# A branch around an attention: the unused side's code moved in front of the used one, and two masks moved inside

## The chip, the cores and the metric

The kernel runs on one core of a Trainium2 chip. The core has five engines that run side by side, each with its own instruction stream: TensorE (PE in the profile; its weight loads are PEld), VectorE (DVE), ScalarE (ACT), GpSimd (POOL) and SyncE (SP), which here only issues transfers. Each engine takes its instructions in order and waits on semaphores for the others. The metric is the device time of one execution in microseconds (us); lower is better.

## What is computed

The reference runs two stages. The first is causal attention with a sliding window and sink tokens, over 4 batches, 8 heads, 768 positions and head size 64; `n_sink` (4) and `window` (128) are inputs that the kernel reads at run time. The second is a mixture of 8 experts with sticky routing: a token keeps the expert of the token before it unless a local gate is below one half.

```python
scores = scale * np.matmul(q, k.transpose(0, 1, 3, 2))
keep = (pos[None, :] < n_sink) | ((rel >= 0) & (rel < window))    # rel = query - key position
a = softmax(np.where(keep, scores, -1e9))
x = np.matmul(a, v)                                               # then heads side by side: [B, S, 512]

for each batch, for each position s:
    fresh_e = argmax(x[s] @ w_gate)
    e = fresh_e if s == 0 or sigmoid(x[s] @ w_local) < 0.5 else prev_e
    out[s] = softmax(x[s] @ w_gate)[e] * (relu(x[s] @ w1[e]) @ w2[e])
```

## The kernel before

**Two attentions, one branch.** Because `n_sink` and `window` are known only at run time, the kernel holds two versions of the attention, both made by `attention(fast)`. The usual one, `attention(True)`, is for narrow masks: a window of 1 to 128 and at most 8 sinks. It looks, for each block of 128 queries, only at the block's own keys, at those of the block before it, and at 8 sink keys. The general one, `attention(False)`, looks at all 768 keys and works for any values. VectorE computes a flag from the two numbers (lines 180 to 191), every engine loads it into a register (`values_load`, line 212), and each engine takes its own branch (`tc.If(narrow != 0)`, line 834). With the inputs of the reference the usual side is taken. Both sides are unrolled code, and both stand one after the other in each engine's instruction stream: the usual one directly behind the branch, the general one behind it. The usual side therefore ends with a jump past the general one. That jump is also recorded under line 834.

**Before the branch.** SyncE and ScalarE issue the first loads (lines 87 to 161); they include queries and keys of the first two head pairs, first their leading 256 columns, then the rest. TensorE runs warm-up matmuls (line 173). VectorE makes three additive masks in one tile (lines 194 to 204): `mask2`, 264 columns wide, for blocks 2 to 5 (keys of the block before, 8 sinks, own keys), `mask1`, 256 columns, for block 1, and `mask0`, 128 columns, for block 0. A kept place has 0 in the mask and every other one -3e38. `rel` is the distance of query and key and `key` the number of the sink key, both loaded tables.

**Splitting queries and keys.** The scores are computed from high and low halves: a number is rounded to the matmul's format (the high half, line 120) and the remainder is the low half (line 125). For each pair of heads `qk_split` gives two steps, keys and queries. In group 0 (`SENG`) the key's high half is VectorE's, its low half GpSimd's, the query's high half ScalarE's and its low half VectorE's. The first pair's leading columns (`lead0[0:2]`) are split ahead of the branch, the second pair's (`lead0[2:]`, line 743) right behind it, and the remaining columns (`rest0`) two steps each at the ends of blocks 0 and 1.

**Inside the usual side.** There are 48 blocks (4 batches, 2 groups of 4 heads, 6 blocks of queries), in a software pipeline with an order written out by hand for TensorE, VectorE and ScalarE (`tc.manual_schedule`); SyncE's and GpSimd's order is left to the scheduler. In step n, block n is scored and evicted, block n-1 is transposed, block n-2 is multiplied with the values, and block n-3 is finished:

- `score` (line 548): six matmuls for each of the two head pairs: high by high, high by low, low by high.
- `out` (lines 560 and 563): for each of a pair's two heads VectorE evicts the scores from PSUM, adds the mask and takes the row's extreme, and ScalarE takes the exponential. `out(now[0])` is the first pair, `out(now[1])` the second.
- `turn` and `turned` (578, 585), `apply` (614), `back` (504) and `finish` (520, 524): transposition, product with the values, and division by the sum.

Routing of a finished batch (lines 248 to 342) is interleaved; its last part, for half of the last batch, comes behind the branch.

**Behind the branch.** The first expert's first 256 tokens are already fetched and transposed at the end of the usual side (`early_prep`, lines 384 to 390: ScalarE's copy is the high half of `x_a`, VectorE's subtraction at line 390 the low half). What follows is common to both sides. TensorE begins with the first layer of expert 0 (line 1000): 24 matmuls for two slices of the hidden size, then the transposes of the late routing (line 280), which need VectorE's `fk` (lines 265 and 266), then more slices. SyncE's first transfer there is a weight load (line 866). The experts are run by a sequence of switches (recorded under line 1295), each a jump to one of 25 unrolled arms.

Of the kernel before, what the change touches and what calls it, by code (L numbers as in the profile page):

```python
# [15 lines left out]
ALU = mybir.AluOpType  # L16
# [3 lines left out]
P = 128  # L20
# [7 lines left out]
SK = 8  # L28
# [5 lines left out]
BIG = 3.0e38  # L34
# [4 lines left out]
N2 = 2 * P + SK  # L39
# [27 lines left out]
def kernel(ctx, tc, qkd, vn, vs, w1, w2, nw, c_misc, c_ident, c_idw, c_small,  # L67
                                          c_all, out):
    nc = tc.nc
# [23 lines left out]
    rel, key = misc[:, 0:N2], misc[:, N2:N2 + SK]  # L93
# [75 lines left out]
    with tc.tile_pool(name="ps_w", bufs=1, space=PS) as ps_w:  # L169
        wt = ps_w.tile([P, 512], F32, name="wt")  # L170
        zb = zrow.bitcast(BF16)
        for _ in range(WARM):
# [11 lines left out]
                                   op0=ALU.mult, op1=ALU.add)  # L184
    nsk, win = scal[:, 0:1], scal[:, 1:2]
# [6 lines left out]
                                             op0=ALU.is_le, op1=ALU.mult)  # L192

    mask = at.tile([P, N2 + 3 * P], F32, name="mask")
    mask2, mask1, mask0 = mask[:, 0:N2], mask[:, N2:N2 + 2 * P], mask[:, N2 + 2 * P:]
    nc.vector.tensor_scalar(mask2, rel, win, None, op0=ALU.is_lt)
    nc.vector.scalar_tensor_tensor(out=mask2, in0=rel, scalar=0.0, in1=mask2, op0=ALU.is_ge, op1=ALU.mult)
    nc.vector.tensor_scalar(mask2[:, P:P + SK], key, nsk, None, op0=ALU.is_lt)
    nc.vector.tensor_copy(mask1[:, 0:P], mask2[:, 0:P])
    nc.vector.tensor_copy(mask1[:, P:2 * P], mask2[:, P + SK:N2])  # L200
    nc.vector.tensor_copy(mask0, mask2[:, P + SK:N2])
    for m in (mask1, mask0):
        nc.vector.tensor_tensor(out=m[:, 0:SK], in0=m[:, 0:SK], in1=mask2[:, P:P + SK], op=ALU.max)
    nc.vector.tensor_scalar(mask, mask, BIG, -BIG, op0=ALU.mult, op1=ALU.add)

    lead0, heads0 = qk_split(0, SENG, False, slice(0, lead), slice(0, lead))
    rest0 = qk_split(0, SENG, False, slice(lead, S), slice(lead, KPAD))[0]
    with tc.issue_after(flag_op.ins) if FLAGF else ExitStack():
        for f in lead0[0:2]:
            f()  # L210

    narrow = nc.values_load(flag_i[0:1, 0:1], min_val=0, max_val=1,
                            skip_runtime_bounds_check_because="a product of comparisons")
# [19 lines left out]
    def setup():  # L233
        nc.sync.dma_start(xs[0:P, :], zrow)
        nc.gpsimd.tensor_copy(identb, ident)
        nc.scalar.copy(base_r, base_f)
# [164 lines left out]
    def xb_meta(b):  # L401
        xb = xb_t[b % 2]
        nc.gpsimd.tensor_copy(xb.bitcast(I32)[:, :, DM + 1], ids[:, b * NBLK:(b + 1) * NBLK])
        nc.gpsimd.memset(xb[:, :, DM + 2:ROW], 0.0)
# [50 lines left out]
    def attention(fast):  # L455
        sfx = "f" if fast else "g"
        with ExitStack() as st:
# [40 lines left out]
            def collect(blk, n):  # L498
                blk["xt"] = t = p2.tile([P, NPR, P], F32, tag="xt", name=f"xt{n}")
                blk["out"] = nc.vector.tensor_copy(t, blk["avt"])  # L500
# [12 lines left out]
            def invert(blk):  # L513
                nc.vector.reciprocal(blk["rs"], blk["rs"])
# [14 lines left out]
            def spans(i):  # L529
                if i == 0:  # L530
                    return P, 0, mask0, ((0, 0),)
                if i == 1:
                    return 2 * P, 0, mask1, ((0, 0), (1, P))
                return N2, koff(i - 1), mask2, ((i - 1, 0), (i, P + SK))

            def score(u):
                b, g, i, c, heads = u["b"], u["g"], u["i"], u["c"], u["heads"]
                w, off, mk, tiles = spans(i)
                n = f"{sfx}{b}_{g}_{i}_{c}"
                if c == 0:  # L540
                    u["blk"]["pe"] = pe_p.tile([P, HG, N2], F32, tag="pe", name=f"pe{n}")
                    u["blk"]["z"], u["blk"]["n"] = sum_z[:, ((b * G + g) * NBLK + i) % NZ], n
                u["bias"] = p3.tile([P, 2], F32, tag="bias", name=f"bias{n}")
                sps = ps_s.tile([P, 2, 512], F32, tag="s", name=f"s{n}")

                for m, (qx, kx) in enumerate(heads[c]):
                    for t in range(2):
                        u["mm"] = nc.tensor.matmul(sps[:, t, :w], qx[ROWS[t], i * P:(i + 1) * P],  # L548
                                                   kx[ROWS[t], off:off + w], start=m == 0, stop=m == 2)
                u["sps"] = sps  # L550

            def out(u):
                i, c = u["i"], u["c"]
                w, off, mk, tiles = spans(i)
                n = f"{sfx}{u['b']}_{u['g']}_{i}_{c}"
                pe, z, bias, sps = u["blk"]["pe"], u["blk"]["z"], u["bias"], u["sps"]
                for t in range(2):
                    h = 2 * c + t
                    sm = p3.tile([P, N2], F32, tag="sm", bufs=4, name=f"sm{n}_{t}")
                    u["dve"] = nc.vector.tensor_tensor_reduce(out=sm[:, :w], in0=sps[:, t, :w], in1=mk, scale=-0.125,  # L560
                                                              scalar=BIG, op0=ALU.add, op1=ALU.min,
                                                              accum_out=bias[:, t:t + 1])
                    nc.scalar.activation(pe[:, h, :w], sm[:, :w], AF.Exp, bias=bias[:, t:t + 1], scale=-1.0,  # L563
                                         accum_out=z[:, h, 0:1])

            def pack(blk, n):
                blk["pk"] = pk = p2.tile([P, 3, HG, SK], F32, tag="pk", name=f"pk{n}")
                nc.vector.tensor_copy(pk, blk["pe"][:, :, P:P + SK].unsqueeze(1).broadcast_to([P, 3, HG, SK]))

            def turn(u):  # L570
                b, g, i, c = u["b"], u["g"], u["i"], u["c"]
                w, off, mk, tiles = spans(i)
                n = f"{sfx}{b}_{g}_{i}_{c}"
                nt, pe = len(tiles), u["blk"]["pe"]
                tp = ps_t.tile([P, 2, 2, P], F32, tag="t", name=f"tp{n}")
                for t in range(2):
                    for k, (j, o) in enumerate(tiles):
                        nc.tensor.transpose(tp[:, t, k, :], pe[:, 2 * c + t, o:o + P], ident)  # L578
                u["tp"] = tp
# [105 lines left out]
            if fast:  # L685
# [62 lines left out]
                for n in range(nb + 3):  # L748
                    now, a, z, y = (blocks[x] if 0 <= x < nb else [] for x in (n, n - 1, n - 2, n - 3))
                    nm = f"{sfx}{n}"  # L750
                    deep = bool(a) and a[0]["i"] >= 2
                    for u in now:
                        if u["k"] == 0 and u["g"] == 0 and n:
                            xb_meta(u["b"])
                        if u["gi"] == 0 and u["k"] == 6:
                            xb_meta(0)
                            setup()
                        u["heads"] = u["prep"]["heads"]
                        score(u)
                    if deep:  # L760
                        pack(a[0]["blk"], nm)
                    if y:
                        collect(y[0]["blk"], nm)
                    if now:
                        out(now[0])
                    for u in a:
                        turn(u)
                    if deep or y:
                        bk = ps_b.tile([P, 512], F32, tag="b", name=f"bk{nm}")
                    if deep:  # L770
                        tps = sink_turn(a[0]["blk"], bk)
                    mm = back(y[0]["g"], y[0]["blk"], bk) if y else None
                    if a:
                        turned(a[0])
                    lo = sink_out(a[0]["blk"], tps, mm, nm) if deep else None
                    if now:
                        out(now[1])
                    if a:
                        turned(a[1])
                        sums(a[0]["blk"])  # L780
                    if y:
                        finish(y[0]["b"], y[0]["g"], y[0]["i"], y[0]["blk"], bk, nm)
                    if deep:
                        lo()
                    if a:
                        invert(a[0]["blk"])
                    if n < 2:
                        for f in rest0[2 * n:2 * n + 2]:
                            f()
                    for u in now:  # L790
                        slot(u, u["gi"], u["k"])
                    if y:
                        done(y[0]["b"], y[0]["g"], y[0]["i"])
                    if z:
                        apply(z, nm)
                    weights(n, now[0] if now else None)
                    for _ in range((ENDING if n >= nb - 2 * NBLK + 2 else STEPS).get(
                            n if n >= nb - 2 * NBLK + 2 else n % (2 * NBLK), 0)):
                        step()
# [31 lines left out]
            while pend:  # L831
                step()

    with tc.If(narrow != 0) as branch:
        attention(True)
    with branch.Else():
        attention(False)
# [461 lines left out]
```

## Time and profile before

| what | us |
|---|---|
| runs shown | 606.99, 608.37, 1598.67 |
| their median | 608.37 |
| time of the profiled execution | 606.81 |
| span of the profiled execution, first to last instruction | 605.0 |
| busy in it: TensorE | 541.8 (90%) |
| VectorE | 354.4 (59%) |
| ScalarE | 284.9 (47%) |
| GpSimd | 233.3 (39%) |

The run of 1598.67 us stands far from the others and is not used for comparisons. The profiled execution lies 0.2 us below the faster of the other two.

Times in the rows of the profile are microseconds from the first instruction of the span. A row of the timeline reads: start, duration, engine, line, operation, what it writes and from what, shapes, how many instructions are merged into the row, and in brackets how long the engine was idle before and what ended this idleness ("<-issue": nothing that the profile shows). An engine's name with a q (SPq, DVEq) is its instruction sequencer. In the view of a single line, a row gives the count, the shortest, median and longest duration in ns, and the first and last start in us. In a view of windows, a row gives the stretch, its length, the busy time and number of instructions of TensorE, its weight loads, VectorE, ScalarE and GpSimd, then the granted TensorE clock, the busy share of the transfer engines and GB/s.

### The profile page before, as it was taken

The page shows a single profiled execution, that of the slowest core. Times are in us where ns is not written, and L with a number is a line of the kernel's source. Part 1 is how long each engine was busy: PE and PEld are TensorE (multiplying, and loading weights), DVE is VectorE, ACT ScalarE, POOL GpSimd, SP SyncE. Part 2 cuts the span into 40 slices and gives each one's busy share as a digit, 9 for nine tenths or more (in the row PEclk, how much of TensorE's full clock was granted, in tenths as well). Part 3 has the DMA queues.
Part 4 walks back from the last instruction along what each step waited for, and adds up shares of the span by engine and source line. Part 5 has one row for each costly group of instructions (what it writes and reads, how often), then busy time and mean ns, then how long its engine had stood idle before and what let it go on. Part 6 is the DMA issues. An engine that isn't in the chain of part 4 may idle for free. (4 is left out here: it accounts for less than half of the span.)

```text
span 605.0 us, 11792 instructions
## 1 busy us (share of the span) xinstructions
PE 541.8 (90%) x3896; PEld 458.8 (76%) x3896; DVE 354.4 (59%) x1288; ACT 284.9 (47%) x850; POOL 233.3 (39%) x188
## 2 busy tenths in 40 slices
PE   6899997989788886779589999989999899999995
PEld 3688786768667765668579978887887679888894
DVE  5677887587758865563736627464454866272321
ACT  2788785578548574222426318161532636132220
POOL 4973370837181064132616106253440355302201
PEclk7699998899799898579679999999999999999999
DMA  8633403252234034138148027484632719211000
GB/s 298 254 105 127 168 12 157 89 186 91 74 137 162 1 117 164 59 106 260 62 117 284 37 74 262 142 282 126 255 122 64 264 66 343 77 39 38 36 22 34
DMA packets 30473, 80.38 MB, mean 133 GB/s; under 512 B 3774, under 2 KB 5310, under 8 KB 30272
## 3 DMA queue, kind: packets, MB, share of 16 engines
q1 hardware_dynamic: 25520, 65.41, 31.4%
q0 software_dynamic: 4176, 12.64, 5.5%
q14 instruction: 148, 1.21, 0.7%
q8 instruction: 53, 0.87, 0.7%
q10 hardware_dynamic: 576, 0.25, 0.1%
HBM read 63.27 MB, written 16.06 MB: 131 GB/s over the span
## 5 line engine op out<-in xcount | busy, mean ns | idle before, releaser
L563 ACT ACTIVATE pef<-smf,biasf 128x264 f32<-128x264 f32 (+2 forms) x192 | 93.6, 489 | 58.8 <-DVE biasf L560 58.8
L560 DVE CUSTOM_DVE_ANT_0 smf<-sf,mask 128x264 f32<-128x264 f32 (+2 forms) x192 | 66.8, 402 | 14.6 <-PE sf L548 7.9
L1011 ACT ACTIVATE hx<-h 128x256 fp32r<-128x256 f32 (+3 forms) x72 | 24.2, 359 | 107.4 <-PE h L1000 91.7
L1049 PE MATMUL late<-w_a,hx 128*128 128x512 f32 (+2 forms) x288 | 68.8, 393 | 1.0 <-issue 1.0
L979 DVE SCALAR_TENSOR_TENSOR hx<-h,hx 128x256 fp32r<-128x256 f32 (+3 forms) x72 | 26.7, 390 | 70.2 <-ACT hx L1011 66.1
L1049 PEld LDWEIGHTS late<-w_a,hx 128*128 128x128 f32 (+2 forms) x288 | 50.7, 179 | 14.5 <-issue 1.5
L578 PE MATMUL tpf<-ident,pef 128*128 128x128 f32 x352 | 56.3, 300 | 2.2 <-ACT ptf L585 2.0
L1049 PE MATMUL late<-w_b,hx 128*128 128x512 f32 (+1 forms) x216 | 55.7, 415 | 2.3 <-DMA xs<-zrun 2.0
L1031 POOL DMA_INDIRECT out_dram<-ot_d,oi_d x18 | 18.7, 1037 | 100.4 <-DVE ot_d L1030 80.2
L614 PE MATMUL avf<-ptf,v 128*64 128x128 f32 x704 | 54.1, 294 | 1.6 <-issue 1.6
L1049 PEld LDWEIGHTS late<-w_b,hx 128*128 128x128 f32 (+1 forms) x216 | 41.6, 196 | 14.0 <-ACT w_b L879 2.1
L585 ACT COPY ptf<-tpf 128x512 f32<-128x512 f32 (+1 forms) x96 | 51.1, 532 | 1.0 <-issue 0.5
L578 PEld LDWEIGHTS tpf<-ident,pef 128*128 128x128 f32 x352 | 40.9, 150 | 12.4 <-ACT ptf L585 5.4
L1011 ACT ACTIVATE hx<-hs 128x96 fp32r<-128x96 f32 (+2 forms) x72 | 16.7, 274 | 70.6 <-DVE hs L994 59.5
L614 PEld LDWEIGHTS avf<-ptf,v 128*64 128x64 f32 x704 | 40.7, 145 | 7.7 <-issue 3.2
L520 DVE TENSOR_TENSOR xb<-bkf,rsf 128x256 f32<-128x256 f32 x48 | 20.3, 423 | 36.4 <-ACT ptsf L595 28.1
L504 PE MATMUL bkf<-idw,xtf 128*128 128x146 f32 x192 | 35.8, 311 | 5.2 <-DVE xtf L500 2.3
L880 POOL TENSOR_TENSOR w_c<-raw,w_c 128x1024 fp32r<-128x1024 f32 x11 | 27.9, 2543 | 31.6 <-ACT w_c L879 26.2
L342 POOL DMA_INDIRECT xs<-xb,slotf x21 | 20.5, 976 | 50.9 <-DVE early_i L362 31.8
L880 POOL TENSOR_TENSOR w_b<-raw,w_b 128x1024 fp32r<-128x1024 f32 x10 | 25.6, 2556 | 36.3 <-ACT w_b L879 27.8
L880 POOL TENSOR_TENSOR w_a<-raw,w_a 128x1024 fp32r<-128x1024 f32 x10 | 26.5, 2650 | 30.2 <-ACT w_a L879 28.1
L548 PE MATMUL sf<-w_a 64*128 64x264 f32 (+2 forms) x288 | 29.2, 325 | 8.3 <-DVE biasf L560 2.2
(228 smaller groups left out, 1146.2 us busy)
## 6 DMA issues: line engine op xcount, KB each, us to landing
raw<-in_dram SPq DMA_DIRECT2D x53, 512.0 KB, 6.0
raw<-in_dram SPq DMA_DIRECT2D x14, 800.0 KB
xr_0n<-xs SPq DMA_DIRECT2D x21, 258.0 KB, 2.7
v<-in_dram SPq DMA_DIRECT2D x7, 768.0 KB, 8.4
raw_w<-in_dram SPq DMA_DIRECT2D x7, 512.0 KB
raw<-in_dram SPq DMA_DIRECT2D x10, 256.0 KB
xs<-zrun SPq DMA_DIRECT2D x9, 258.0 KB
xr_0r<-xs SPq DMA_DIRECT2D x8, 258.0 KB, 3.1
```

Source lines behind the costliest of these rows:

```text
L342: s_i = nc.gpsimd.indirect_dma_start(out=xs[:, :], out_offset=bass.IndirectOffsetOnAxis(ap=slot[:, j:j + 1].bitcast(U32), axis=0), in_=xb[ ...
L504: mm = nc.tensor.matmul(bk[:, pr * WX:(pr + 1) * WX], blk["xt"][:, pr, :], idw[:, g * NPR + pr, :], start=True, stop=True, skip_group_chec ...
L548: u["mm"] = nc.tensor.matmul(sps[:, t, :w], qx[ROWS[t], i * P:(i + 1) * P], kx[ROWS[t], off:off + w], start=m == 0, stop=m == 2)
L560: u["dve"] = nc.vector.tensor_tensor_reduce(out=sm[:, :w], in0=sps[:, t, :w], in1=mk, scale=-0.125, scalar=BIG, op0=ALU.add, op1=ALU.min, ...
L563: nc.scalar.activation(pe[:, h, :w], sm[:, :w], AF.Exp, bias=bias[:, t:t + 1], scale=-1.0, accum_out=z[:, h, 0:1])
L578: nc.tensor.transpose(tp[:, t, k, :], pe[:, 2 * c + t, o:o + P], ident)
L585: nc.scalar.copy(pt[:, :, 0:nt, :], tp[:, :, 0:nt, :])
L614: nc.tensor.matmul(avt[ROWS[t], pr, :], prep["v"][:, j, 2 * pr + t, :], x["pt"][:, t, k, :], start=i < 2 and pr == 0 and k == 0, stop=pr = ...
L880: todo += [lambda s=s: lo(out=l[:, s], in0=raw[:, s], in1=h.bitcast(F32)[:, s], op=ALU.subtract) for s in ([slice(0, FF)] if eng[1] == "po ...
L979: nc.vector.scalar_tensor_tensor(out=d[:, :, 1, :], in0=h, scalar=0.0, in1=d.bitcast(F32)[:, :, 0, :], op0=ALU.max, op1=ALU.subtract)
L1011: relu = nc.scalar.activation(d[:, :, 0, :], h, AF.Relu)
L1049: nc.tensor.matmul(o, a, w, start=t == 0, stop=t == len(mm) - 1, skip_group_check=half)
```

## The change

Two things are changed.

First, the branch gets `preferred_fallthrough_block=False`. The general attention's code now stands directly behind the branch and the usual one's behind it. The branch to the usual side now has to go past the general code, and the end of the usual side runs on into the common code with no jump.

Second, ahead of the branch VectorE makes only `mask0`, in four instructions on 128 or 8 columns. The two wider masks are made inside, by `wide_masks()`, which VectorE's hand-written order calls once, in step 0, between the evictions of block 0's first head pair (two evictions) and those of its second. There the mask of 264 columns is scaled before `mask1` is copied from it. No wait and no transfer is added, and the values of the masks are the same.

```diff
-    nc.vector.tensor_scalar(mask2, rel, win, None, op0=ALU.is_lt)
-    nc.vector.scalar_tensor_tensor(out=mask2, in0=rel, scalar=0.0, in1=mask2, op0=ALU.is_ge, op1=ALU.mult)
-    nc.vector.tensor_scalar(mask2[:, P:P + SK], key, nsk, None, op0=ALU.is_lt)
-    nc.vector.tensor_copy(mask1[:, 0:P], mask2[:, 0:P])
-    nc.vector.tensor_copy(mask1[:, P:2 * P], mask2[:, P + SK:N2])
-    nc.vector.tensor_copy(mask0, mask2[:, P + SK:N2])
-    for m in (mask1, mask0):
-        nc.vector.tensor_tensor(out=m[:, 0:SK], in0=m[:, 0:SK], in1=mask2[:, P:P + SK], op=ALU.max)
-    nc.vector.tensor_scalar(mask, mask, BIG, -BIG, op0=ALU.mult, op1=ALU.add)
+    nc.vector.tensor_scalar(mask0, rel[:, P + SK:N2], win, None, op0=ALU.is_lt)
+    nc.vector.scalar_tensor_tensor(out=mask0, in0=rel[:, P + SK:N2], scalar=0.0, in1=mask0, op0=ALU.is_ge,
+                                   op1=ALU.mult)
+    nc.vector.scalar_tensor_tensor(out=mask0[:, 0:SK], in0=key, scalar=nsk, in1=mask0[:, 0:SK], op0=ALU.is_lt,
+                                   op1=ALU.max)
+    nc.vector.tensor_scalar(mask0, mask0, BIG, -BIG, op0=ALU.mult, op1=ALU.add)
+
+    def wide_masks():
+        nc.vector.tensor_scalar(mask2, rel, win, None, op0=ALU.is_lt)
+        nc.vector.scalar_tensor_tensor(out=mask2, in0=rel, scalar=0.0, in1=mask2, op0=ALU.is_ge, op1=ALU.mult)
+        nc.vector.tensor_scalar(mask2[:, P:P + SK], key, nsk, None, op0=ALU.is_lt)
+        nc.vector.tensor_scalar(mask2, mask2, BIG, -BIG, op0=ALU.mult, op1=ALU.add)
+        nc.vector.tensor_copy(mask1[:, 0:P], mask2[:, 0:P])
+        nc.vector.tensor_copy(mask1[:, P:2 * P], mask2[:, P + SK:N2])
+        nc.vector.tensor_tensor(out=mask1[:, 0:SK], in0=mask1[:, 0:SK], in1=mask2[:, P:P + SK], op=ALU.max)
...
                     if now:
                         out(now[0])
+                    if not n:
+                        wide_masks()
                     for u in a:
                         turn(u)
...
-    with tc.If(narrow != 0) as branch:
+    with tc.If(narrow != 0, preferred_fallthrough_block=False) as branch:
         attention(True)
     with branch.Else():
         attention(False)
```

## The prediction

> **What bounds the kernel now.** I read the page first, for the span, then the view of the branch's own line, because the change moves code around exactly one branch. L834 is the branch at the entry of the attention and also the jump that ends its usual side.
>
> ```profile
> span 605.0 us, 11792 instructions
> ```
> ```profile
> L834 PEldq COMPARE_BRANCH  x2: 83/2492/4902, 5.7 to 243.5; - x2
> L834 POOLq COMPARE_BRANCH  x2: 41/43/45, 6.1 to 245.3; - x2
> L834 ACTq COMPARE_BRANCH  x2: 43/46/49, 6.2 to 246.0; - x2
> L834 SPq COMPARE_BRANCH  x2: 38/44/49, 7.2 to 227.5; - x2
> L834 DVEq COMPARE_BRANCH  x2: 50/54/57, 8.6 to 246.7; - x2
> ```
>
> Each engine has two records: one at the entry (5.7 to 8.6 us) and one at the exit (227.5 to 246.7 us). TensorE's took 83 ns at the entry, where the usual code stands right behind the branch, and 4902 ns at the exit, where it must get past the general code. The other engines' records are short, and the price shows as idle time behind them. Next I read the timeline of the exit, engine by engine:
>
> ```profile
> 248.57 5.46 PE L1000 MATMUL h_s<-x_a,w_a 128*128 128x256 f32 x24 [2.57 <-issue]
> 253.96 0.63 PE L280 MATMUL tfs<-identb,fk 128*8 128x128 bf16 x6
> ```
> ```profile
> 246.03 0.58 ACT L387 CAST x_a<-xpfe 128x512 fp32r<-128x512 f32 x1 [0.27 <-PE xpfe L384]
> ...
> 246.65 0.69 DVE L390 TENSOR_TENSOR x_a<-xpfe,x_a 128x512 fp32r<-128x512 f32 x1
> 249.93 0.54 DVE L248 TENSOR_REDUCE lgs<-lw 128x27 f32<-128x216 f32 x1 [2.59 <-issue]
> ...
> 251.68 0.17 DVE L266 TENSOR_SCALAR fk<-frs 128x24 bf16<-128x24 f32 x1
> ```
> ```profile
> 228.29 6.06 SPq L866 DMA_DIRECT2D raw<-in_dram  x3
> ```
>
> "<-issue" means that the engine waited for nothing the profile shows. TensorE stands 2.57 us and VectorE 2.59 us in this way right behind the jump; VectorE's gap from branch (246.7) to next instruction (249.93) is 3.2 us. SyncE, whose general code is short, issues a load within 0.8 us of its jump (227.5 to 228.29). So a jump over the general code is dear on TensorE (4.9) and VectorE (3.2), and cheap on SyncE. Last I read the start, where the same jump will stand:
>
> ```profile
> 5.45 0.35 DVE L196 TENSOR_SCALAR mask<-misc,scal 128x264 f32<-128x264 f32 x1
> 5.71 0.94 DVE L125 TENSOR_TENSOR w_a<-raw,w_a 128x256 fp32r<-128x256 f32 x1
> 6.58 0.42 DVE L197 SCALAR_TENSOR_TENSOR mask<-misc,mask 128x264 f32<-128x264 f32 x1
> 7.04 0.23 DVE L198 TENSOR_SCALAR mask<-misc,scal 128x8 f32<-128x8 f32 x1
> 7.18 0.22 DVE L199 COPY mask<-mask 128x128 f32<-128x128 f32 x1
> 7.31 0.22 DVE L200 COPY mask<-mask 128x128 f32<-128x128 f32 x1
> ...
> 7.58 0.29 DVE L203 TENSOR_TENSOR mask<-mask 128x8 f32<-128x8 f32 x2
> 7.90 0.50 DVE L204 TENSOR_SCALAR mask<-mask 128x648 f32<-128x648 f32 x1
> 8.72 0.29 DVE L120 CAST w_a<-raw 128x256 fp32r<-128x256 f32 x1 [0.32 <-DVE mask L204]
> 8.93 0.42 DVE L125 TENSOR_TENSOR w_a<-raw,w_a 128x256 fp32r<-128x256 f32 x1
> 9.27 0.28 DVE L560 CUSTOM_DVE_ANT_0 smf<-sf,mask 128x128 f32<-128x128 f32 x1
> ...
> 11.62 0.29 DVE L560 CUSTOM_DVE_ANT_0 smf<-sf,mask 128x128 f32<-128x128 f32 x1 [1.85 <-PE sf L548]
> ...
> 13.37 1.23 DVE L125 TENSOR_TENSOR w_a<-raw,w_a 128x512 fp32r<-128x512 f32 x1 [0.89 <-ACT w_a L120]
> 14.53 0.41 DVE L560 CUSTOM_DVE_ANT_0 smf<-sf,mask 128x256 f32<-128x256 f32 x1
> ```
> ```profile
> 5.98 1.06 PE L548 MATMUL sf<-w_a 64*128 64x128 f32 x6
> ...
> 10.86 2.33 PE L548 MATMUL sf<-w_a 64*128 64x128 f32 x16 [1.22 <-POOL w_a L125]
> ```
> ```profile
> 12.74 0.60 ACT L120 CAST w_a<-raw 128x512 fp32r<-128x512 f32 x1
> ```
> ```profile
> 10.08 0.73 POOL L125 TENSOR_TENSOR w_a<-raw,w_a 128x256 fp32r<-128x256 f32 x1
> ...
> 12.86 0.39 POOL L492 CAST srf<-sxf 96x256 fp32r<-96x256 f32 x1 [2.06 <-DMA sxf<-in_dram]
> ```
>
> The start is a chain, not a throughput. VectorE makes the key's high half for the second pair of heads only behind the masks (8.72); GpSimd's low half waits on it and on its own work (10.08); TensorE's second score group waits for that (10.86); its eviction comes at 11.62. From there exponentials, the split of the remaining query columns on ScalarE (12.74), its low half on VectorE (13.37) and block 1's evictions (14.53) follow one another. I see no slack between these, so I count a delay of the 11.62 eviction in full to the end of the attention.
>
> **The change part by part.**
>
> *Exit.* The jump goes. What is late next is the row L390, which ends 246.65 + 0.69 = 247.34; the low half it writes is read by the second matmul of L1000, and the first needs only ScalarE's copy (246.03 + 0.58 = 246.61). TensorE may start between these and 248.57: a gain of 1.23 by the later, 1.96 by the earlier row, and 0 if another wait takes its place. I take 1.3: almost everything hangs on the later row, with one matmul ahead of it. VectorE's 2.59 us is worth nothing of its own: what it makes for TensorE (fk, done 251.68 + 0.17 = 251.85) is used at 253.96, behind 24 matmuls, so 2.1 us of slack hide it. If that cover went, it would be worth at most 1.3 more. ScalarE's next work needs TensorE's first product. SyncE and GpSimd are far ahead or idle there.
>
> *Masks before the branch.* VectorE loses L196 to L204, which run from 6.58 to 8.40 behind L125, and L196's 0.26 (5.45 to 5.71) ahead of it. It gains four instructions on 128 or 8 columns. By the rows: 0.22 (as L199's 128 columns) ahead of L125; then about 0.29 for the two-operand form (between half and all of L197's 0.42), 0.15 for the 8-column maximum (half of L203's 0.29) and 0.22. So it ends near 6.6 + 0.29 + 0.15 + 0.22 = 7.3, not 8.40. The branch came at 8.6, 0.7 behind the start of the last mask instruction (7.90); the last now starts near 7.05, so the branch stands near 7.7.
>
> *The jump at the entry.* It is taken now, over the same general code. VectorE: 7.7 + 3.2 = 10.9, where its first instruction inside stood at 8.72. TensorE: 5.7 + 4.9 = 10.6, first matmul 10.8 (it was 5.98), first group of six done near 11.8. ScalarE's jump can't be told from its wait at the exit; with VectorE's 3.2 it arrives at 9.4, ahead of need. SyncE: under 0.8, as at the exit. If it paid 3.2, the transfers it issues first inside (sinks, the next raw tiles and values) would be late; the sinks hold up GpSimd's 12.86 row and the key's low half behind it, and beside a chain already 2.4 late this is about 1 more. GpSimd would arrive at 6.1 + 3.2 = 9.3 at worst, ahead of its 10.08 row: 0. Bounds for VectorE's jump: 0 (as at the entry now, 8.6 to 8.72) and 5.0, from
>
> ```profile
> L1295 PEldq COMPARE_BRANCH  x16: 298/2168/4960, 283.8 to 588.2; - x16
> ```
>
> the longest jump among the arms of the second half. I take VectorE's own, 3.2.
>
> *Inside.* VectorE: high half 10.9 to 11.1 (8.72 to 8.93 now), then L125, 0.94 as at 5.71 because GpSimd makes its low half beside it, to 12.0. Evictions of the first pair take 0.45 (9.27 and its partner), to 12.45. Then the wide masks: 0.26 (L196), 0.46 (6.58 to 7.04), 0.14 (7.04 to 7.18), about 0.30 for the scaling of 264 columns (between L196's 0.35 and its spacing of 0.26), 0.13 twice (7.18 to 7.31), 0.15: together 1.57, to 14.0. The second pair's scores: GpSimd's low half ends near 12.0, four matmuls at 2.33/16 = 0.15 each and their drain give 12.8. So of the masks' 1.57 some 0.35 lie beside TensorE's work and 1.2 are on the path. The eviction of 11.62 stands at 14.0: 2.4 later. What waits behind the masks on VectorE: that eviction, ScalarE's two exponentials, and through them the query split. Bounds: with a jump of 0 VectorE arrives at 7.8, GpSimd still works at 10.08, and the masks fit into the 1.85 us hole ahead of 11.62: cost 0. With 5.0 the path is 1.8 longer: 4.2.
>
> *Sum.* The profiled execution took 606.81 us (span 605.0). 606.81 + 2.4 - 1.3 = 607.9; I say 608.0. The undisturbed runs shown are 606.99 and 608.37; the listed median, 608.37, is the higher of these, the third, 1598.67, being no run to compare with. On a session that sits at 608.4 the same sum would read 609.5.
>
> **A rule against this sum.** The granted clock of three stretches of the start:
>
> ```profile
> 6.00:20.00 14.00, 7.65 (x41) 5.10 (x41) 9.60 (x36) 5.92 (x22) 8.68 (x14) 0.59 1.04 395
> ...
> 22.17:25.58 3.41, 3.41 (x25) 2.84 (x24) 2.24 (x11) 2.16 (x9) 3.41 (x4) 0.50 0.02 5
> 25.58:28.99 3.41, 3.41 (x41) 2.95 (x40) 1.85 (x8) 2.40 (x8) 3.33 (x3) 1.00 0.93 332
> ```
> ```profile
> 20.00 1.97 PE L578 MATMUL tpf<-ident,pef 128*128 128x128 f32 x8
> ```
>
> The last three numbers of a row of windows are the granted clock, the share of the transfer engines that was busy, and GB/s. TensorE works without a break from 20.0, at half clock to 25.58 and at full clock behind it. If the clock is raised only behind a whole busy stretch of 3.41 us with fixed edges, work that begins at 22.4 misses the edge at 22.17 and the raise comes at 28.99: 6.6 us at half clock for 5.6, half of the difference lost, 0.5 us. The Trainium skill, "TensorE: Matmul & The Clock Gate", Part 1, says so: a free-running window of 4096 cycles, some 3.4 us, decides. The two rows agree with it for this one edge.
>
> **Rivals.**
> - *Window edge:* the mechanism just priced, 608.0 + 0.5 = 608.5. For it: the rows above. Against it: where the edges lie in another execution is not shown. 0.12.
> - *Entry hidden:* the entry costs 0 because the jump at the entry is short or the chain has slack I don't see; 606.81 - 1.3 = 605.5. For it: SyncE gets over its general code in under 0.8 us, so such a jump can be cheap. Against it: 4902 ns on TensorE and 3.2 us on VectorE over the very code that they will jump over. 0.15.
> - *Long jump:* VectorE pays 5.0: 606.81 + 4.2 - 1.3 = 609.7, about 611 if SyncE misses too. For it: the transfers are full at the entry (share 1.04 in the row 6 to 20). 0.11.
> - *Starved fetch, the slower side:* code comes by transfers of its own, on the page a queue by itself,
>
> ```profile
> q14 instruction: 148, 1.21, 0.7%
> ```
>
> and such a transfer could stand behind the loads, which keep the engines of all queues full to 20 us. VectorE then arrives at 20 and not at 10.9, so 9.1 more: 617, and beyond 619 (slower by over 2%) if the fetch needs more than 22 us. It decides from there. Against it:
>
> ```profile
> L1295 PEldq COMPARE_BRANCH  x1: 4960/4960/4960, 420.4 to 420.4; - x1
> ```
> ```profile
> 420.40:425.40 5.00, 4.09 (x18) 2.95 (x16) 0.00 (x0) 0.00 (x0) 0.68 (x1) 1.00 0.79 249
> ```
>
> TensorE's longest jump of the second half, 4960 ns, ran there, at a transfer share of 0.79, with no sign of standing behind the loads. 0.03.
>
> **How the numbers follow.** The forecast has the rest, 0.59: 606.5 to 609.5 with the 1.6 us between the executions shown. The range takes in the hidden entry and the long jump with SyncE's miss: 605.3 to 611.2. What a measurement of this kernel tells from no change is about 2%, 12 us; only the starved fetch reaches it. Faster 0.01, same 0.97, slower 0.02.
>
> **What would show it.** Exit: no record of L834 there, TensorE's L1000 within 0.2 us of L390's end, VectorE's L248 right behind L390. Entry: VectorE's first L120 inside near 10.9 and TensorE's first L548 near 10.8, both with idle time put down to issue. Masks: seven mask instructions on VectorE between the first two and the next two L560, about 1.6 us, with TensorE's second group done ahead of them. The second pair's eviction near 14.0, block 1's near 16.9. The prediction is wrong if the jump at the entry is much shorter than at the exit, if block 1's eviction comes back to 14.5, or if the span shrinks by more than the exit's 1.3.

## The result and the profile after

| | us |
|---|---|
| before, median (in the same comparison) | 606.40 |
| changed kernel, median | 613.60 |
| ratio, with its 95% interval | 1.0107 [1.0082, 1.0132] |
| profiled execution of the changed kernel, time and span | 614.78, 613.0 |

The changed kernel is slower by about 6.5 us ((1.0107 - 1) x 606.4; interval 5.0 to 8.0); the two medians lie 7.2 us apart. That is under 2%, as forecast. But 608.0 was predicted and the range ended at 611.2: scaled to the execution from which the sum was made, the measured time is 606.81 x 1.0107 = 613.3, and its interval begins at 611.8. One disturbed run of the kernel before (1598.67 us) is left out of the ratio.

The view of the branch's line, which is now L842 (below it L554, L566, L396 and L1008 are the old L548, L560, L390 and L1000):

```profile
L842 PEldq COMPARE_BRANCH  x1: 5997/5997/5997, 5.8 to 5.8; - x1
L842 ACTq COMPARE_BRANCH  x1: 50/50/50, 5.9 to 5.9; - x1
L842 POOLq COMPARE_BRANCH  x1: 50/50/50, 5.9 to 5.9; - x1
L842 SPq COMPARE_BRANCH  x1: 50/50/50, 6.9 to 6.9; - x1
L842 DVEq COMPARE_BRANCH  x1: 67/67/67, 7.6 to 7.6; - x1
```

One record for each engine is left. The exit has none, and TensorE's at the entry has become 5997 ns. VectorE's timeline:

```profile
6.91 0.23 DVE L201 TENSOR_SCALAR mask<-mask 128x128 f32<-128x128 f32 x1
13.34 0.29 DVE L120 CAST w_a<-raw 128x256 fp32r<-128x256 f32 x1 [6.20 <-DMA v<-in_dram]
13.55 0.42 DVE L125 TENSOR_TENSOR w_a<-raw,w_a 128x256 fp32r<-128x256 f32 x1
13.88 0.29 DVE L566 CUSTOM_DVE_ANT_0 smf<-sf,mask 128x128 f32<-128x128 f32 x1
...
14.30 0.40 DVE L204 TENSOR_SCALAR mask<-misc,scal 128x264 f32<-128x264 f32 x1
14.74 0.51 DVE L205 SCALAR_TENSOR_TENSOR mask<-misc,mask 128x264 f32<-128x264 f32 x1
15.28 0.58 DVE L206 TENSOR_SCALAR mask<-misc,scal 128x8 f32<-128x8 f32 x1
15.90 0.30 DVE L207 TENSOR_SCALAR mask<-mask 128x264 f32<-128x264 f32 x1
16.23 0.76 DVE L208 COPY mask<-mask 128x128 f32<-128x128 f32 x1
16.90 0.85 DVE L209 COPY mask<-mask 128x128 f32<-128x128 f32 x1
17.67 0.15 DVE L210 TENSOR_TENSOR mask<-mask 128x8 f32<-128x8 f32 x1
17.75 0.28 DVE L566 CUSTOM_DVE_ANT_0 smf<-sf,mask 128x128 f32<-128x128 f32 x1
...
33.90 0.42 DVE L566 CUSTOM_DVE_ANT_0 smf<-sf,mask 128x264 f32<-128x264 f32 x1
```

The branch stands at 7.6 (7.7 was predicted), the first instruction inside at 13.34 (10.9 was predicted). The profile puts the idle time down to a transfer of `v`, which L120 does not read; with the usual layout and the same masks ahead, the same L120 runs at 7.55 (experiment 2), so its data were there and the wait, 5.8 from the branch, is the jump. The second pair's eviction is at 17.75, where it was 11.62 before and 14.0 predicted: 6.1 later and not 2.4. How the missing 3.75 comes about can be read off these rows: the jump took 2.44 more than predicted (13.34 for 10.9); the split and the first two evictions took 0.59 less (13.34 to 14.30, for 10.9 to 12.45); the masks took 1.90 more (14.30 to 17.75 = 3.45, for 1.55). GpSimd's timeline shows what ran beside the masks:

```profile
14.50 0.46 POOL L498 CAST srf<-sxf 96x256 fp32r<-96x256 f32 x1
15.04 0.80 POOL L499 TENSOR_TENSOR srf<-sxf,srf 32x256 fp32r<-32x256 f32 x1
15.90 1.78 POOL L120 CAST qk_b<-raw 128x800 fp32r<-128x800 f32 x2
```

The eight columns of L206 took 0.58 (0.23 for L198 before) and ended at 15.86, with GpSimd's L499 (15.84). The copies took 0.76 and 0.85 (0.22 before), and the second ended at 17.75, with GpSimd's two casts (17.68).

How far the delay goes on is seen at block 4, whose first eviction in the kernel before was here:

```profile
28.70 0.42 DVE L560 CUSTOM_DVE_ANT_0 smf<-sf,mask 128x264 f32<-128x264 f32 x1
```

The changed kernel's row stands at 33.90: 5.2 later. That is less than 6.1, because the clock was raised only 3.4 later. Two windows of the changed kernel, and then the ends of its attention on TensorE and on VectorE:

```profile
25.60:29.00 3.40, 3.40 (x18) 2.58 (x20) 2.07 (x11) 2.44 (x8) 3.40 (x3) 0.50 0.10 9
29.00:32.40 3.40, 3.40 (x41) 2.94 (x39) 2.29 (x12) 2.73 (x11) 3.32 (x3) 1.00 0.92 344
```
```profile
255.06 1.19 PE L1008 MATMUL h_s<-x_a,w_a 128*128 128x256 f32 x4 [1.49 <-DVE x_a L396]
```
```profile
254.22 0.69 DVE L396 TENSOR_TENSOR x_a<-xpfe,x_a 128x512 fp32r<-128x512 f32 x1
254.95 0.55 DVE L254 TENSOR_REDUCE lgs<-lw 128x27 f32<-128x216 f32 x1
```

The exit is as predicted: TensorE starts 0.15 behind the low half (254.22 + 0.69 = 254.91), and VectorE's next instruction follows at once.

### The profile page after: what moved, and what is told of

It is laid out like the page before. It is cut to its first block, busy times and chain, and to the rows that moved or that the text cites. A ratio compares the mean times of both kernels' runs of the same rounds, so it can differ in the third digit from the quotient of the medians.

```text
span 613.0 us, 11790 instructions
## 1 busy us (share of the span) xinstructions
PE 540.0 (88%) x3896; PEld 459.7 (75%) x3896; DVE 356.3 (58%) x1290; ACT 285.2 (47%) x850; POOL 234.1 (38%) x188
## 5 line engine op out<-in xcount | busy, mean ns | idle before, releaser
L566 DVE CUSTOM_DVE_ANT_0 smf<-sf,mask 128x264 f32<-128x264 f32 (+2 forms) x192 | 66.8, 402 | 14.3 <-remote 7.6
L1057 PEld LDWEIGHTS late<-w_b,hx 128*128 128x128 f32 (+1 forms) x216 | 41.6, 195 | 13.4 <-ACT hx L1019 2.1
L554 PE MATMUL sf<-w_a 64*128 64x264 f32 (+2 forms) x288 | 29.2, 326 | 16.7 <-issue 9.2
L554 PEld LDWEIGHTS sf<-w_a 64*128 64x128 f32 x288 | 22.4, 207 | 23.2 <-issue 12.4
## 6 DMA issues: line engine op xcount, KB each, us to landing
v<-in_dram SPq DMA_DIRECT2D x7, 768.0 KB, 10.4
```

The source lines that it names most:

```text
L1057: nc.tensor.matmul(o, a, w, start=t == 0, stop=t == len(mm) - 1, skip_group_check=half)
```

## The experiments

"Excess" is (ratio - 1) times the median of the kernel before in the same comparison; it is to be compared with "block 4", which is how much later than 28.70 block 4's first eviction started in the profiled execution (left out for 11).

| experiment | ratio, 95% | excess, us | block 4, us |
|---|---|---|---|
| the change | 1.0107 [1.0082, 1.0132] | 6.5 | 5.2 |
| 1 layout alone | 1.0128 [1.0077, 1.0180] | 7.7 | 4.8 |
| 2 masks alone | 1.0047 [1.0006, 1.0089] | 2.8 | 2.7 |
| 3 the change, timed again | 1.0129 [1.0095, 1.0163] | 7.8 | 5.6 |
| 4 the change, quiet entry | 1.0044 [1.0007, 1.0080] | 2.7 | 3.0 |
| 5 the change, hint | 1.0098 [1.0071, 1.0125] | 6.0 | 7.4 |
| 6 masks alone, GpSimd's old order | 0.9993 [0.9962, 1.0023] | -0.4 | -0.8 |
| 7 layout alone, hint | 1.0065 [1.0037, 1.0093] | 4.0 | 5.4 |
| 8 the change, hint, old order | 1.0115 [1.0076, 1.0154] | 7.0 | 6.6 |
| 9 before, a pause at the entry | 1.0122 [1.0071, 1.0173] | 7.3 | 6.0 |
| 10 before, an earlier start | 1.0029 [0.9994, 1.0064] | 1.7 | 0.8 |
| 11 before, unchanged | 0.9984 [0.9944, 1.0023] | -1.0 | - |

**1 and 2: each half alone.** Experiment 1 is the kernel before with the flag of the branch alone, experiment 2 the changed kernel without it.

```diff
-    with tc.If(narrow != 0) as branch:
+    with tc.If(narrow != 0, preferred_fallthrough_block=False) as branch:
```

> The general code in front, all masks where they were. Theory: the jump at the entry costs VectorE 5.7 us as in the changed kernel (7.6 to 13.34), here from 8.6 to 14.3; the second pair's first eviction comes near 16.2 (11.62 before, 17.75 in the changed kernel), 4.6 late, and the exit gives 1.1 back: 3.5 us slower than before, ratio 1.006. Rival, that the masks and not the jump make the loss: within 1 us of before.

The layout alone costs as much as the whole change. VectorE's first row inside:

```profile
14.47 0.29 DVE L120 CAST w_a<-raw 128x256 fp32r<-128x256 f32 x1 [6.08 <-DMA v<-in_dram]
```

The branch stood at 8.5, the jump took 5.9, and the second pair's eviction came at 16.50, 4.9 late, much as expected. The masks are ahead of the branch here, so the masks' place is not what costs most. The whole was expected to lose 3.5 and lost 7.7 [4.6, 10.8].

> The wide masks inside, behind two evictions; the usual code directly behind the branch as before. Theory: with no jump VectorE arrives inside near 7.7, GpSimd's low half still starts near 10.1, and the masks fall into the hole ahead of the second pair's eviction: that eviction between 11.6 and 12.1, the time within 0.5 us of before. Rival, that the masks in this place cost by themselves what they took in the changed kernel beyond their 1.6 us: 2 us slower.

Here the second pair came at 11.41, a little earlier than before (11.6 to 12.1 was expected), since the masks fit into the hole. Yet the kernel is slower, by a cost whose cause no theory had. GpSimd's rows, then TensorE's:

```profile
17.39 1.88 POOL L125 TENSOR_TENSOR qk_b<-raw,qk_b 128x800 fp32r<-128x800 f32 x1
19.22 2.08 POOL L120 CAST qk_b<-raw 128x800 fp32r<-128x800 f32 x2
21.27 1.32 POOL L125 TENSOR_TENSOR w_a<-raw,w_a 128x544 fp32r<-128x544 f32 x1
```
```profile
22.64 0.81 PE L554 MATMUL sf<-w_a 64*128 64x264 f32 x4 [4.13 <-POOL w_a L125]
```

And GpSimd in the kernel before:

```profile
17.54 1.33 POOL L125 TENSOR_TENSOR w_a<-raw,w_a 128x544 fp32r<-128x544 f32 x1
18.83 2.34 POOL L125 TENSOR_TENSOR qk_b<-raw,qk_b 128x800 fp32r<-128x800 f32 x1
```

No instruction of GpSimd was edited, but its order is left to the scheduler. The low half for block 2 (`w_a`, 544 columns) slid from 17.54 to 21.27, behind work for the next group of heads (`qk_b`), and TensorE waited 4.13 for it.

**6: is it the order?** Experiment 2 with the old order held by dependences that add no wait on another engine:

```diff
+    def after_low(i, n):
+        tc.add_manual_dep(i.ins, pool_low[n].ins.name, mybir.DependencyInfo(
+            mybir.DependencyClass.NoSync, mybir.DependencyReason.DATA), reason="GpSimd's order")
...
```

> The masks alone, with GpSimd's order at the start put back to that of the kernel before (the low half of the second pair's remaining key columns ahead of the next group's products). Theory, that the masks alone lost 3.4 us because that low half had slid behind three instructions of the next group: TensorE's wait of 4.13 us for it goes, block 2's second pair is evicted near 20.2 (23.50 with the masks alone, 20.11 before), block 3 near 24.0, and the time is within 1 us of before, ratio 0.998 to 1.002. Rival, that the masks' own instructions make the loss: block 3 near 27.4, ratio 1.005.

Block 2's second pair came at 19.60 (23.50 in experiment 2) and the excess went. So the masks' new place by itself costs nothing that shows when the entry is on time; the scheduler's order did.

**4: the jump with quiet transfers.** The changed kernel, with 1.9 MB of loads (the table `idw`, the remaining query and key columns, the rest of the values) held until TensorE's first matmul inside the branch:

```diff
-    nc.sync.dma_start(idw.rearrange("p r c -> p (r c)"), c_idw)
-    qk_load(0, slice(lead, KPAD))
-    qk_load(1, slice(lead, KPAD))
-    nc.sync.dma_start(v_t[0][:, 2:NBLK], vn[0, 0, :, 2:NBLK])
...
+                        if not n and u is now[0]:
+                            late_loads(u["mm"])
```

> The changed kernel with 1.9 MB of the first loads (the projection, the remaining columns of queries and keys, the remaining values) held until TensorE's first score matmul inside, so that the transfer engines are nearly idle during the jump. Theory, that full transfers make the jump long: VectorE's gap from branch to first instruction 3.2 to 4.0 us (5.7 in the changed kernel), TensorE's jump below 5.0 (6.0). Rival, that the entry's jump is long for another reason: 5.7 and 6.0 again. The time by itself says little, since the remaining columns come late: 4 to 9 us slower than before.

The branch's line, VectorE's timeline and the window of the jump (the last three numbers: clock, share of the transfer engines, GB/s), and last the same window of the changed kernel:

```profile
L853 PEldq COMPARE_BRANCH  x1: 3351/3351/3351, 5.6 to 5.6; - x1
...
L853 DVEq COMPARE_BRANCH  x1: 67/67/67, 7.3 to 7.3; - x1
```
```profile
10.69 0.29 DVE L120 CAST w_a<-raw 128x256 fp32r<-128x256 f32 x1 [3.79 <-issue]
...
13.58 0.23 DVE L216 COPY mask<-mask 128x128 f32<-128x128 f32 x1
13.72 0.22 DVE L217 COPY mask<-mask 128x128 f32<-128x128 f32 x1
```
```profile
6.00:11.00 5.00, 1.19 (x8) 0.44 (x6) 1.14 (x5) 0.40 (x1) 0.89 (x6) 0.95 0.44 101
```
```profile
6.00:11.00 5.00, 0.00 (x0) 0.00 (x0) 1.07 (x4) 0.00 (x0) 0.77 (x6) 0.75 1.01 373
```

At a share of 0.44 instead of 1.01 TensorE's jump took 3.35 (5.997 in the changed kernel) and VectorE's 3.4 (7.3 to 10.69; 5.8 in the changed kernel): the price of the exit. But for a few loads it is the same general code, jumped over at the same place, so the transfers make the difference. The view of the transfers shows where: a row gives queue, kind, packets, MB and share of the transfer engines, and "instruction" packets are code. First the changed kernel from 9.2 to 11.8, then experiment 4 from 5.5 to 9.0:

```profile
q14 instruction: 4, 0.03, 3.8%
q8 instruction: 1, 0.02, 2.4%
```
```profile
q14 instruction: 4, 0.03, 3.8%
q8 instruction: 1, 0.02, 1.7%
```

These are the first code packets behind TensorE's branch. The changed kernel has none from 5.7 to 9.2; the first starts at 9.3, 3.5 behind that branch. In experiment 4 the first starts at 6.5, 0.9 behind it. The packets themselves take about as long in both (1.0 and 0.9 for the one on q8), so they start late and are not slower. The kernel before, where the usual code stands behind the branch, has none from 5.7 to 13.4. Which packet belongs to which engine the view does not tell. The Trainium skill, "Runtime: NRT & Kernel Launch", Instruction fetch mechanics, says that a taken branch out of the prefetched window has to wait until its target has been fetched by DMA. These rows agree. The second pair came at 13.94; block 1 then waited for the loads held back, so the 2.7 us of excess are not the price of the jump alone. The masks' two copies took 0.23 and 0.22 with GpSimd idle beside them.

**3, 5, 7: the jump's fetch announced.** Three kernels with a hint at the start of the program that the branch will be taken. In experiment 3 the hint named no engines and left no instruction, so it is a second timing of the changed kernel:

```diff
+    tc.mark_branch_hint_location("usual", "LikelyTaken")
...
```

> The changed kernel with a hint ahead of the first loads that tells TensorE, ScalarE and VectorE to fetch the usual code. If the kernel is the one with the hint on all three engines: theory, that the loss is the fetch at the entry: the jumps shrink below 1 us, the start goes as with the masks alone, the exit gives 1.1: 0.7 to 1.1 us faster than before, ratio 0.998. Rival, that the hint does nothing because the fetch is not what the engines wait for: 1.0107 as the changed kernel.

It repeats the result (7.8 us) and the entry: VectorE's L120 at 13.16. In experiment 5 the hint names three engines, and in experiment 7 it is added to experiment 1:

```diff
+    tc.mark_branch_hint_location("usual", "LikelyTaken", engines=[ET.PE, ET.Activation, ET.DVE])
...
```

> The changed kernel with one prefetch hint each on TensorE, ScalarE and VectorE at the start of the program, for the branch's usual side. Theory, that the loss at the entry is the fetch of far code: VectorE's gap from branch to first instruction falls from 5.7 us to under 1, TensorE's jump from 6.0 to under 1; the start then goes as in the run with the masks alone (block 3's first eviction near 27.4, 3.4 late, because GpSimd's order is the same), the exit gives 1.1: about 2.3 us slower than before, ratio 1.004. Rival, that a hint this early does nothing: gap 5.7, ratio 1.011.

> The layout alone (masks and GpSimd's order as before) with the hint on the three engines. Theory: the entry as before (second pair's eviction at 11.6, block 3 at 24.0), the exit 1.1 shorter: 1.1 us faster than before, ratio 0.998. Rival, that the layout costs beyond the jump: 1.005 or more.

The branch's line and VectorE in experiment 5:

```profile
L843 PEldq COMPARE_BRANCH  x1: 495/495/495, 6.0 to 6.0; - x1
```
```profile
14.37 0.29 DVE L120 CAST w_a<-raw 128x256 fp32r<-128x256 f32 x1 [6.98 <-DMA v<-in_dram]
```

TensorE's jump all but went (0.5), VectorE's stayed at 6.6 from its branch at 7.8, and at 5.9 in experiment 7; so did the delay at block 4 (7.4 and 5.4). VectorE's jump sets the delay, and not TensorE's. The view of experiment 5's transfers from 0 to 6, ahead of the branch, has one code packet that the changed kernel does not have there:

```profile
q8 instruction: 1, 0.02, 1.4%
```

The packets on q14 did not move ahead of the branch: the first stands at 9.4, where the changed kernel had its first at 9.7. So the hint brought a part of the code early, and the rest came as late as without it. Why it does so for TensorE and not for VectorE stays open.

**8: GpSimd's order with a late entry.** Experiment 5 with the order of experiment 6.

> The changed kernel with the hint on the three engines and GpSimd's order put back. Theory: no part of the loss is left, the second pair's eviction near 11.4, block 3 near 24.0, the exit 1.1 shorter: 0.998. Rival, that something else of the change costs: 1.003 or more.

The masks took 2.3 (14.98 to 17.27, 3.4 in experiment 5), because GpSimd was idle beside the two copies (0.23 and 0.22, for 0.75 and 0.85 beside its casts). Of the 1.5 won at the second pair (17.27, 18.78 in experiment 5), 1.0 was left at block 2 (25.86, 26.90), and the whole remained as slow: 7.0 [4.6, 9.4], 6.0 [4.3, 7.6] in experiment 5. With a late entry GpSimd's order decides about the masks' duration, but no gain of it shows at the end.

**9: a pause in place of the jump.** The kernel before, exit jump and all, with nine additions behind the branch that nobody reads (VectorE, 128x512), and GpSimd's order held:

```diff
+                pause = p2.tile([P, 512], F32, tag="pause", bufs=1, name="pause")
+                for _ in range(PAUSE):
+                    nc.vector.tensor_tensor(out=pause, in0=mask[:, 0:512], in1=mask[:, 0:512], op=ALU.add)
...
```

> The kernel before with nine additions of 512 columns that nothing reads (about 0.65 us each, 5.8 us together) on VectorE right behind the branch, GpSimd's order held as it was. Theory, that VectorE's late arrival at the entry goes to the end in full: the second pair's eviction near 16.5, block 3's first near 29.8 (24.02 before), the time 5.8 us longer, ratio 1.008 to 1.011. With the exit's jump still in place this is also what the changed kernel would cost if the exit gave nothing. Rival, that part of the delay is made up later in the attention: ratio below 1.006.

```profile
8.35 6.49 DVE L762 TENSOR_TENSOR pause<-mask 128x512 f32<-128x512 f32 x9 [0.32 <-DVE mask L217]
...
16.77 0.29 DVE L575 CUSTOM_DVE_ANT_0 smf<-sf,mask 128x128 f32<-128x128 f32 x1 [0.97 <-PE sf L563]
```

The delay of 16.77 - 11.62 = 5.2 at the second pair was 6.0 at block 4 and 7.3 [4.3, 10.4] at the end. A late start of VectorE is enough for the whole result, without the new layout; and the exit jump, which this kernel keeps, does not show: TensorE started 0.14 behind the low half.

**10 and 11: can the masks' part be used alone?** Experiment 10 has the old layout, the wide masks behind both pairs' evictions and the next split, and GpSimd's low halves first.

```diff
-                        for f in rest0[2 * n:2 * n + 2]:
+                        for k, f in enumerate(rest0[2 * n:2 * n + 2]):
...
+                            if not n and not k:
+                                wide_masks()
...
```

> The usual code directly behind the branch as before, the wide masks inside but behind both pairs' evictions and one split, and GpSimd's two low halves of the first group's second pair and rests ahead of its other work there. Theory, that the start is a chain through VectorE and GpSimd's low halves: the second pair's eviction near 9.6 (11.62 before), block 3 near 22.0 (24.0 before), 1 to 2 us faster than before, ratio 0.997. Rival, that the chain is held by loads: block 3 at 24 and ratio 1.000.

> The kernel before against itself, unchanged. Ratio 1.000, interval over 1. In its profile the jump at the exit is looked at again: if TensorE's loss behind the end of the low half is 1.2 us as in the first profile, the exit's gain is as large as forecast; in two other runs with this layout it was 0.14 and 0.43.

In experiment 10 the second pair's eviction came at 9.66, 2.0 earlier than before, and the gain was lost again by block 2 (21.30, 19.35 before). VectorE, then GpSimd:

```profile
10.83 1.46 DVE L216 SCALAR_TENSOR_TENSOR mask<-misc,mask 128x264 f32<-128x264 f32 x1
...
13.27 0.69 DVE L132 TENSOR_TENSOR w_a<-raw,w_a 128x512 fp32r<-128x512 f32 x1
...
17.48 3.90 DVE L132 TENSOR_TENSOR w_a<-raw,w_a 128x512 fp32r<-128x512 f32 x1 [1.53 <-ACT w_a L120]
```
```profile
10.61 1.39 POOL L132 TENSOR_TENSOR w_a<-raw,w_a 128x544 fp32r<-128x544 f32 x1 [0.76 <-DVE w_a L120]
...
17.65 3.19 POOL L120 CAST qk_b<-raw 128x800 fp32r<-128x800 f32 x4
```

The same subtraction took 0.69 with GpSimd idle and 3.90 beside GpSimd's casts, which had moved there; the mask's L216 took 1.46 (0.42 as L197 before) beside GpSimd's low half. The whole was 1.7 us slower [-0.4, 3.8], where 1 to 2 us of gain were expected. Run again beside it, the kernel before (experiment 11) lay within 0.2% of itself. No version was found that beats the kernel before.

## Why the prediction was wrong, step by step

- *The jump at the entry* is the step that failed. The mechanism was right: the price moves from exit to entry, VectorE's share counts, SyncE's is small (0.5). But the price was taken from VectorE's own row at the exit, 3.2, and the entry is where the transfers are full. It was 5.8 there, above the bound of 5.0 too, which came from TensorE. Experiment 4 gave the exit's price back (3.4) by taking the transfers away. The prediction had the share of 1.04 in front of it and used it for two rivals, at 0.11 and 0.03, and not for the forecast. Of the rivals the long jump (609.7 to 611) was the nearest; its place and direction were right, with VectorE at 5.8 and not 5.0, but without a miss on SyncE. The starved fetch named the mechanism, but would have held VectorE to 20; it stood at 13.34.
- *The masks* were mis-sized: 1.57 by spacings read where GpSimd was idle, 3.45 measured. The prediction itself set L125 at 0.94 "because GpSimd makes its low half beside it" and did not ask the same of the seven instructions behind it. Experiments 5 and 8 show the copies at 0.75 and 0.85 beside GpSimd's casts and at 0.23 and 0.22 without. The Trainium skill, "SBUF — State Buffer", Who interferes with whom, says that VectorE and GpSimd share one pair of ports, and that the loser waits for the other's whole instruction; L206 and L209 of the changed kernel, which end within 0.1 of GpSimd's rows, agree. Experiment 10's long subtraction fits less simply: its row starts 0.17 ahead of the first of four casts and ends 0.54 behind the last.
- *First split inside:* 0.94 predicted, 0.42 measured, as GpSimd's low half started behind it (0.59 to the good, with the evictions).
- *Full pass-through* held as far as can be told: 6.1 at the second pair, 5.2 at block 4, 6.5 [5.0, 8.0] at the end; experiment 9 gave 5.2, 6.0 and 7.3 [4.3, 10.4]. Between block 4 and the end it rests on the ratios. Two single executions no longer show it there: the attention's last low half (L390 before) came 7.6 later in the changed kernel, and 0.6 earlier in experiment 1, whose excess was 7.7.
- *Window edge:* the clock's raise did move by one whole step of 3.4 (25.58 to 29.00), so the rule is borne out for this edge, but with the sign turned: the second pair was 6.1 later and the raise only 3.4, and by block 4 0.9 of the delay had gone.
- *The exit's 1.3* was read from one execution, and the others do not bear it out. In the kernel before TensorE's jump began at 243.5 and took 4.9, and 3.84 of that lay beside the work that leads to the low half (247.34). In experiment 2, with the same exit code, it took 3.9:

```profile
L842 PEldq COMPARE_BRANCH  x2: 83/1978/3872, 5.6 to 245.6; - x2
```
```profile
248.84 0.69 DVE L396 TENSOR_TENSOR x_a<-xpfe,x_a 128x512 fp32r<-128x512 f32 x1
```
```profile
249.67 2.69 PE L1008 MATMUL h_s<-x_a,w_a 128*128 128x256 f32 x11 [1.49 <-DVE x_a L396]
```

  It ended at 249.5, as the low half did (248.84 + 0.69 = 249.53), and TensorE began 0.14 behind: the jump was hidden. So it was in experiment 11, the kernel before itself, where the jump began at 240.6 and took 3.7, the low half ended at 244.59, and TensorE began 0.15 behind:

```profile
244.74 4.45 PE L1000 MATMUL h_s<-x_a,w_a 128*128 128x256 f32 x24 [1.49 <-DVE x_a L390]
```

  Experiments 9 and 10 gave 0.14 and 0.22. Experiment 6 had a jump of 3.4 that began closer to the low half's end, and a gap of 0.43. Without the jump the gap is 0.15, in the changed kernel as in experiment 1. So the exit was worth 1.1 in one of six executions, the one from which the prediction was made, and 0.3 or less in the other five; the lower bound of 0 should have weighed more. In the table the excess minus the delay at block 4 is 0.5 on the mean of the seven kernels without the exit jump, and 0.7 on that of experiments 2, 6, 9 and 10, which have it: the runs show no gain of its removal, and could not show one well below 1 us.
- *Not foreseen:* GpSimd's order. Behind a late entry no cost of it shows (experiment 8).

With the measured entry (6.1) and an exit of 0, the same sum gives 606.81 + 6.1 = 612.9, with an exit of 1.1 611.8, and 613.3 [611.8, 614.8] was measured.

## What to carry to other kernels

A far jump should be priced by the traffic of the place to which it moves, and a jump that overlaps with the last work before it may cost nothing there. Work that is moved on VectorE should be laid against GpSimd's timeline, instruction by instruction, before its old durations are used. After any edit one should look whether an engine whose order is left to a scheduler still makes first what is needed first.

## What the runs showed of the hardware

- The same jump took 3.4 (VectorE) and 3.35 (TensorE) at a transfer share of 0.44, and 5.8 and 6.0 at 1.01. The first code packet came 0.9 behind TensorE's branch in the one case and 3.5 in the other. SyncE's jump over its few instructions took 0.5.
- A hint at the program's start cut TensorE's jump from 6.0 to 0.5, and left VectorE's at 5.9 to 6.6; one code packet came ahead of the branch.
- One and the same VectorE subtraction of 128x512 took 0.69 to 3.90, by what GpSimd did beside it.
- Single executions of one kernel differ by more than most of these effects: 19 runs of the kernel before lie between 603.65 and 611.79. Early rows of the trace, and ratios over several rounds, told the kernels apart; the spans of single profiles did not (experiment 10's was 596.0).
